# Recurrence feeding a mixture of experts: bonus sums in half as many products, loads cut into pieces and asked for later, and another order of the matmuls in a chunk

## The chip, the cores and the metric

The program runs on 1 core of one Trainium2 chip. The metric is the device time in microseconds (us) of one execution; lower is better.

## What is computed

A linear recurrence over 768 tokens in 4 batches of 8 heads of width 48, and then a mixture of 8 experts with top-1 routing on its output. Cut to what matters:

```
for t in range(S):                                  # attention, per batch and head
    cur = outer(u * k[t], v[t])
    y[t] = r[t] @ (state + cur)                     # (r*u*k) . v is the "bonus"
    state = w[:, None] * state + outer(k[t], v[t])
x = y laid out as 3072 tokens x 384
e = argmax(x @ w_gate); gate = softmax(x @ w_gate)[e]
out[token] = gate * (relu(x @ w1[e]) @ w2[e])       # each expert takes at most 768 tokens
```

## The kernel before

The 3072 tokens are cut into 24 chunks of 128 (`NI`), 6 for each batch, and each chunk into two halves `s` of 64 tokens. Two heads share the 128 partitions (`g`), four such pairs `p` make up the 8 heads. Inside a chunk the recurrence is done with matrix products; one loop, `for i in range(NI)` (L616), works on several chunks at once. It is written out by hand in the order in which every engine takes its instructions. An iteration `i` does, on TensorE:

- `scores(i + 1)` (L396): 16 products of 64 x 64 into the bank `pk`; VectorE then puts them under the diagonal of the tile `s` (`masks`, L405).
- `turn(i - 1)` (L469): three 128 x 128 transposes of the finished chunk `x` (`xpose`, L73) and the three router products of the chunk before that (`gates`, L77), into one bank `xp` of PSUM. ScalarE copies that bank to SBUF (L486).
- `update(i + 1)` (L408): 16 products for the state, into `pu`. VectorE and GpSimd carry the state on (`carry`, L417: L425, L428, L430).
- `advance("t", 1)`: now and then the products of a routing step (`route`, L111: L120, L121, L158).
- `values(i)` (L432): 16 products of the scores with v, into `py`.
- `fill(i, 4)` (L464): four bf16 products of zeros, 128 x 392, into the bank `xp` that `turn(i)` uses in the next iteration. Their results are overwritten.
- `bonus(i + 3)` (L361): for each pair of heads, half and head one product of a 48 x 64 block of `z` = r*k with one column of u; 16 products of one column each, into a corner of the bank `pu`.
- `inter(i)` (L443): 16 products of r with the state, added to `py`. ScalarE copies `py` to the tile `x` (L456), SyncE stores `x` to DRAM two iterations later (`store`, L459).

ScalarE's order in an iteration: copy of the bonus sums (`bon`, L373), eight multiplications that put them on the diagonal of `s` (`diag`, L377), copy of `xp` (L486), a two-column copy `seen` (L446), copy to `x` (L456), and sometimes a cast of expert 0's weights (L219). GpSimd makes `z` (`product`, L355), the state's multiplication (L430) and `kt` (`prep_state`, L389). VectorE makes `kd` and `rt` (L387, L382).

Loads are asked for by SyncE, which takes its transfers strictly in order. `load(i + 5)` (L346) opens the iteration: r and k of a chunk in two transfers to `dm` (4 buffers), k and v in token order in one to `bd` (6 buffers, L353). The transfer to `bd` reuses the buffer that `values(i - 1)` reads. Behind it stand the store of `x` and, in seven of the iterations, a 384 or 512 KB piece of expert 0's weights (`wstream`, L205, L211), and `dm` of the next chunk. In the built program each SyncE transfer also waits for the transfer eight before it.

Before the loop stand constants (`powers`, L526), the loads of five chunks and some runs of filling products (`warm`, L500). After the loop come expert 0's first layer while the last routing steps end, and then the experts one after the other (L265 to L284); nothing of this part changes.

Of the kernel before, what the change touches and what calls it, by code (L numbers as in the profile page):

```python
# [35 lines left out]
def rwkv_moe(nc, tc, dmj, rkv, bdc, wp, wv, uv, wg, w1, w2, out, cap):  # L36
# [3 lines left out]
    with ExitStack() as ctx:  # L40
# [70 lines left out]
        def route(gi, i0, n, l, sm, ps, tp):  # L111
# [74 lines left out]
        with ExitStack() as mc:  # L186
# [18 lines left out]
            def wstream(e, plan):  # L205
                raw = {}

                def fetch(k):
                    r = raw[k] = wrw.tile([128, F if k < 3 else 2 * DM], F32, tag="wr", name=f"wr{k}_{e}")
                    src = w1[e, :, k] if k < 3 else w2[e, :, 2 * k - 6:2 * k - 4].rearrange("p f d -> p (f d)")  # L210
                    nc.sync.dma_start(out=r, in_=src)  # L211
# [117 lines left out]
            wc = wk.tile([PR, NP], F32, name="wc", bufs=1)  # L329
            w128 = wk.tile([PR, NP], F32, name="w128", bufs=1)  # L330
# [8 lines left out]
            pb = pu[:, :, NP * D:NP * D + NP]  # L339
            ftp = pu[0:PR, :, 256:].rearrange("q h (p t) -> q h p t", p=2)  # L340
            xl_ = wk.tile([128, RING, 392], F32, name="xl_", bufs=1)
# [4 lines left out]
            def load(i):  # L346
                b, c = divmod(i, NC)
                t = T[i] = {"dm": dmb[i % 4]}
                q = 64 if i < 4 else D
# [11 lines left out]
            def bonus(i):  # L361
                t = T[i]
                for p in range(NP):
                    for s in range(2):
                        for g in range(2):
                            r, o = slice(64 * g, 64 * g + D), 64 * (g ^ s)
                            nc.tensor.matmul(pb[o:o + 64, s, p:p + 1], lhsT=t["z"][r, p, 64 * s:64 * s + 64],  # L367
                                             rhs=wut[r, 1, p:p + 1], start=True, stop=True)

            def diag(i):  # L370
                t = T[i]
                bon = sm.tile([128, 2, NP], F32, tag="bon", name=f"bon{i}")
                nc.scalar.copy(out=bon, in_=pb)  # L373
                s = t["s"] = wk.tile([128, 2, NP, 64], F32, tag="s", name=f"s{i}", bufs=3)
                for h in range(2):
                    for p in range(NP):
                        nc.scalar.mul(out=s[:, h, p], in_=eye, mul=bon[:, h, p:p + 1])  # L377
# [560 lines left out]
```

## Time and profile before

| | before |
|---|---|
| median of 3 runs | 456.41 us (452.42 to 460.54) |
| the profiled execution | 449.77 us, its span 448.1 us |
| TensorE: matmuls, weight loads | busy 419.6 us (94%), 375.1 us (84%) |
| VectorE, ScalarE, GpSimd | 231.3 us, 191.6 us, 145.8 us |
| data moved | 59.44 MB, mean 133 GB/s |
| mean granted TensorE clock | 0.871 of full speed |

The granted clock has two levels, 1.00 (2.4 GHz) and 0.50 (1.2 GHz). PE is TensorE's matmuls, PEld its weight loads, DVE VectorE, ACT ScalarE, POOL GpSimd, SPq SyncE's queue. A product in f32 is recorded as two matmuls, so the 16 products of a step stand there as x32. In brackets behind a row stands the idle time ahead of it and what ended it; "issue" is time in which the engine waited for nothing that the profile shows.

### The profile page before, as it was taken

How to read it: one execution, taken by the hardware profiler on the slowest of the kernel's cores; microseconds unless marked ns; L12 is line 12 of the kernel's file. 1: busy time of each engine (PE TensorE's matmuls, PEld its weight loads, DVE VectorE, ACT ScalarE, POOL GpSimd, SP SyncE). 2: the span in 40 equal slices, each digit the busy share in tenths (PEclk: the TensorE clock that was granted, in tenths of full speed). 3: DMA queues.
4: the chain of work that ended last, by engine and by line, in shares of the span. 5: the costliest groups of instructions: out<-in, count | busy, mean ns of one | idle time of the engine just before them, and what ended most of it. 6: DMA issues, size and time to landing. Idle time of an engine off the chain costs nothing.

```text
span 448.1 us, 13332 instructions
## 1 busy us (share of the span) xinstructions
PE 419.6 (94%) x5572; PEld 375.1 (84%) x5573; DVE 231.3 (52%) x518; ACT 191.6 (43%) x545; POOL 145.8 (33%) x228
## 2 busy tenths in 40 slices
PE   8779998899987998879999999999999999999994
PEld 4458787778776877778999999999999999999993
DVE  5525534357566696378556445365463553553320
ACT  4425355335353544327337245264263462552402
POOL 4742525362663354026033131330330420200303
PEclk9855569565596599969999999999999999999998
DMA  7966556463464512208545355444553553430101
GB/s 191 239 161 186 163 161 179 136 169 102 140 188 147 146 45 79 68 18 309 159 145 157 102 185 149 143 137 111 158 152 123 147 161 118 123 92 0 53 0 64
DMA packets 22038, 59.44 MB, mean 133 GB/s; under 512 B 3946, under 2 KB 7058, under 8 KB 21968
## 3 DMA queue, kind: packets, MB, share of 16 engines
q1 hardware_dynamic: 18240, 48.85, 39.0%
q0 software_dynamic: 3584, 9.44, 6.1%
q8 instruction: 46, 0.75, 0.8%
q14 instruction: 24, 0.20, 0.1%
q10 hardware_dynamic: 144, 0.20, 0.1%
HBM read 49.38 MB, written 9.78 MB: 132 GB/s over the span
## 4 chain that ended last, share of the span: by engine, by line
PE 64%; issue 21%; DVE 6%; POOL 4%; ACT 3%; POOLq 1%; DVEq 0%
PE b L282 5%; PE xp L467 5%; PE a L266 5%; PE a L265 5%; PE a L267 5%; PE b L283 5%; PE b L284 5%; PE pu L367 4%; PE py L453 4%; PE xp L77 4%; POOL out L291 3%; PE pu L414 3%; PE py L440 3%; PE xp L73 3%; PE pk L402 3%
## 5 line engine op out<-in xcount | busy, mean ns | idle before, releaser
L265 PE MATMUL a<-xh,ws 128*128 128x412 f32 (+1 forms) x216 | 76.1, 352 | 0.1
L220 DVE TENSOR_TENSOR ws<-wr,ws 128x384 fp32r<-128x384 f32 (+1 forms) x112 | 66.5, 612 | 15.0 <-ACT ws L219 14.0
L266 PE MATMUL a<-xl,ws 128*128 128x412 f32 (+1 forms) x216 | 73.4, 340 | 0.5 <-DVE xl L253 0.5
L267 PE MATMUL a<-xh,ws 128*128 128x412 f32 (+1 forms) x216 | 73.1, 338 | 0.0
L282 PE MATMUL b<-hh,ws 128*128 128x412 f32 (+1 forms) x192 | 68.1, 355 | 0.0
L270 ACT ACTIVATE hh<-a 128x412 fp32r<-128x412 f32 (+2 forms) x72 | 34.3, 476 | 77.2 <-PE a L267 77.2
L291 POOL DMA_INDIRECT out<-yo,ids x32 | 31.2, 976 | 109.0 <-ACT yo L290 109.0
L283 PE MATMUL b<-hl,ws 128*128 128x412 f32 (+1 forms) x192 | 65.8, 343 | 0.0
L284 PE MATMUL b<-hh,ws 128*128 128x412 f32 (+1 forms) x192 | 65.7, 342 | 0.0
L271 DVE SCALAR_TENSOR_TENSOR hl<-a,hh 128x412 fp32r<-128x412 f32 (+2 forms) x72 | 38.7, 538 | 46.5 <-ACT hh L270 46.4
L219 ACT CAST ws<-wr 128x384 fp32r<-128x384 f32 (+1 forms) x112 | 59.8, 557 | 0.0
L234 POOL DMA_INDIRECT xg<-x_dr,ids x30 | 30.0, 999 | 87.9 <-PE tp L248 68.2
L285 DVE COPY yt<-b 128x412 f32<-128x412 f32 (+1 forms) x24 | 13.7, 570 | 72.7 <-PE b L284 72.7
L377 ACT ACTIVATE s<-eye,bon 128x64 f32<-128x64 f32 x192 | 48.5, 335 | 0.8
L266 PEld LDWEIGHTS a<-xl,ws 128*128 128x128 f32 x216 | 41.8, 193 | 1.0 <-DVE xl L253 0.9
L265 PEld LDWEIGHTS a<-xh,ws 128*128 128x128 f32 x216 | 41.8, 194 | 0.8 <-ACT xh L252 0.4
L267 PEld LDWEIGHTS a<-xh,ws 128*128 128x128 f32 x216 | 41.6, 193 | 0.1
L456 ACT COPY x<-py 128x384 f32<-128x384 f32 x24 | 11.5, 478 | 64.7 <-PE py L453 55.3
L430 POOL TENSOR_TENSOR st<-q,w 112x192 f32<-112x192 f32 x20 | 11.9, 597 | 83.2 <-DVE q L428 46.1
L359 POOL TENSOR_TENSOR z<-dm 112x256 f32<-112x256 f32 x48 | 35.2, 755 | 6.8 <-DMA dm<-dmj 5.2
L282 PEld LDWEIGHTS b<-hh,ws 128*128 128x128 f32 x192 | 36.1, 188 | 0.9
L406 DVE COPY_PREDICATED s<-msk,pk 128x512 f32<-128x512 int32 x24 | 17.7, 736 | 36.6 <-PE pk L402 31.7
(145 smaller groups left out, 691.5 us busy)
## 6 DMA issues: line engine op xcount, KB each, us to landing
wr<-w SPq DMA_DIRECT2D x24, 512.0 KB, 3.6
wr<-w SPq DMA_DIRECT2D x32, 384.0 KB, 3.4
bd<-bdc SPq DMA_DIRECT2D x24, 384.0 KB, 3.6
dm<-dmj SPq DMA_DIRECT2D x44, 192.0 KB, 5.6
x_dr<-x SPq DMA_DIRECT2D x23, 192.0 KB, 3.6
dm<-dmj SPq DMA_DIRECT2D x4, 256.0 KB, 8.2
out<-yo,ids POOLq DMA_INDIRECT x32, 2.8
xg<-x_dr,ids POOLq DMA_INDIRECT x30, 3.3
```

The costliest lines, as they stand in the source:

```text
L219: nc.scalar.copy(out=hi, in_=r)
L220: nc.vector.tensor_tensor(out=lo, in0=r, in1=hi.bitcast(F32), op=ALU.subtract)
L265: nc.tensor.matmul(o, lhsT=wh, rhs=xh[:, d, a:z], start=d == 0, stop=False)
L266: nc.tensor.matmul(o, lhsT=wh, rhs=xl[:, d, a:z], start=False, stop=False)
L267: nc.tensor.matmul(o, lhsT=wl, rhs=xh[:, d, a:z], start=False, stop=d == 2)
L271: nc.vector.scalar_tensor_tensor(out=hl[:, f, b:z], in0=o[:, b - a:], scalar=0.0, in1=hh[:, f, b:z].bitcast(F32), op0=ALU.max, op1=ALU.sub ...
L282: nc.tensor.matmul(o, lhsT=wh, rhs=hh[:, f, :n], start=f == 0, stop=False)
L283: nc.tensor.matmul(o, lhsT=wh, rhs=hl[:, f, :n], start=False, stop=False)
L284: nc.tensor.matmul(o, lhsT=wl, rhs=hh[:, f, :n], start=False, stop=f == 7)
L291: r = nc.gpsimd.indirect_dma_start(out=out[:, :], out_offset=bass.IndirectOffsetOnAxis(ap=ids[:q, at:at + 1], axis=0), in_=yo, in_offset=N ...
L359: nc.gpsimd.tensor_tensor(out=z[:, p:p + 2], in0=t["dm"][:, 0, p:p + 2], in1=t["dm"][:, 1, p:p + 2], op=ALU.mult)
L377: nc.scalar.mul(out=s[:, h, p], in_=eye, mul=bon[:, h, p:p + 1])
```

## The change

The bonus sums are made by 8 products in place of 16: all 112 partitions of `z` (both heads) times two columns (`uz`, u of one head in each, zeros elsewhere). For that the layout of r and k on the host swaps the halves of the second head, and the tiles that depend on it (`ft`, `kb`, `s`) are indexed to fit. The sums go to eight columns of the bank `xp` next to the transposes, and the one copy of that bank (400 columns in place of 392) takes them along; the copy `bon` falls away, except for the first four chunks, which have a bank and a copy of their own. `turn` no longer follows `fill` by an iteration: three filling products of 400 columns, the transposes and the router products now come in a row, behind `update`. The copy of the bank follows `bonus` (`keep_turn`). Loads come in six transfers for each chunk (four of 96 KB to `dm`, two of 192 KB to `bk` and `bv`), each where the buffer that it fills has been read, up to seven chunks ahead; expert 0's weights come in halves of 64 partitions, at most two in an iteration. `x` is stored one iteration after it is made. A routing step of the first groups waits one iteration more before its products (`yield "v"`). The setup makes the powers of w in a tile of their own (some small VectorE instructions more).

```
+            if i0 + n < SNAP:
+                yield "v"
...
+                        later.extend([(r[64 * h:64 * h + 64], src[64 * h:64 * h + 64]) for h in range(2)])
...
-                nc.sync.dma_start(out=t["dm"][0:q], in_=dmj[b, c, 0:q])
-                nc.sync.dma_start(out=t["dm"][64:PR], in_=dmj[b, c, D:])
-                bd = t["bd"] = ld.tile([128, 2, 8, D], F32, tag="bd", name=f"bd{i}", bufs=6)
-                nc.sync.dma_start(out=bd, in_=bdc[b, c])
...
+                if j < 2:
+                    q = 64 if i < 4 else D
+                    nc.sync.dma_start(out=t["dm"][0:q, j], in_=dmj[b, c, j, 0:q])
+                    nc.sync.dma_start(out=t["dm"][64:PR, j], in_=dmj[b, c, j, D:])
+                else:
+                    k, bufs = (("bk", 4), ("bv", 6))[j - 2]
+                    n = t[k] = ld.tile([128, 8, D], F32, tag=k, name=f"{k}{i}", bufs=bufs)
+                    nc.sync.dma_start(out=n, in_=bdc[b, c, j - 2])
...
-            def bonus(i):
...
+            def bonus(i, o):
+                z = T[i]["z"]
                 for p in range(NP):
-                    for s in range(2):
-                        for g in range(2):
-                            r, o = slice(64 * g, 64 * g + D), 64 * (g ^ s)
-                            nc.tensor.matmul(pb[o:o + 64, s, p:p + 1], lhsT=t["z"][r, p, 64 * s:64 * s + 64],
-                                             rhs=wut[r, 1, p:p + 1], start=True, stop=True)
+                    for h in range(2):
+                        q = slice(64 * h, 64 * h + 64)
+                        nc.tensor.matmul(o[q, 2 * p:2 * p + 2], lhsT=z[:, p, q], rhs=uz[:, p], start=True, stop=True)
+
+            def bonus_alone(i):
+                m = ps1.tile([128, 8], F32, tag="xp", name=f"pb{i}")
+                bonus(i, m)
+                b = T[i]["bon"] = sm.tile([128, 8], F32, tag="bon", name=f"bon{i}", bufs=4)
+                nc.scalar.copy(out=b, in_=m)
...
-                bon = sm.tile([128, 2, NP], F32, tag="bon", name=f"bon{i}")
-                nc.scalar.copy(out=bon, in_=pb)
...
-                m = turns[i] = ps1.tile([128, 392], F32, tag="xp", name=f"xp{i}")
+            def turn(i, n):
+                m = T.setdefault(i, {})["m"] = ps1.tile([128, 400], F32, tag="xp", name=f"xp{i}")
...
-                    nc.tensor.matmul(m, lhsT=wz[:, 0:128], rhs=wz[:, 0:392], start=True, stop=True)
...
+                hi = 8
+                if i < NI:
+                    hi = 392
+                if i + 4 < NI:
+                    hi = 400
+                    T[i + 4]["bon"] = xl_[:, k, 384:392]
...
             for i in range(NI):
-                each(load, i + 5)
-                if i >= 2:
-                    store(i - 2, nc.sync)
+                if i >= 1:
+                    store(i - 1, nc.sync)
+                part()
                 each(product, i + 3)
                 each(diag, i + 2)
                 each(scores, i + 1)
+                each(update, i + 1)
                 if i >= 1:
-                    turn(i - 1)
-                each(update, i + 1)
+                    turn(i - 1, 3)
                 each(masks, i + 1)
                 each(prep_k, i + 3)
+                each(load, i + 7, 1)
                 each(carry, i + 1)
                 each(prep_r, i + 3)
+                each(prep_state, i + 3)
+                each(load, i + 7, 2)
+                each(load, i + 7, 0)
+                part()
                 advance("t", 1)
                 values(i)
-                fill(i, 4)
-                each(bonus, i + 3)
+                each(load, i + 6, 3)
+                if i >= 1:
+                    if i + 3 < NI:
+                        bonus(i + 3, T[i - 1]["m"][:, 392:])
+                else:
+                    bonus_alone(3)
+                seen(i)
+                if i >= 1:
+                    keep_turn(i - 1)
                 inter(i)
-                each(prep_state, i + 3)
                 advance("v")
                 if i >= 1:
                     next(more, None)
...
                 next(ws)
```

TensorE in one iteration of the loop before (the products of chunks 11 and 12; `xp_2044` is the bank that the next iteration's transposes go to):

```order
L77 MATMUL xp_1904<-wgs,xl__139 128x8 x3
L414 MATMUL pu<-bd_1412,kt_1805 48x48 x16
L440 MATMUL py<-bd_1278,s_1699 64x48 x16
L467 LDWEIGHTS wz
L467 MATMUL xp_2044<-wz 128x392
...
L367 MATMUL pu<-wut,z_1966 64x1 x16
L453 MATMUL py<-st_12_1881,rt_118 64x48 x8
L402 MATMUL pk<-rt_120,kd_124 64x64 x16
L73 MATMUL xp_2044<-idn,x_2075 128x128 x3
L77 MATMUL xp_2044<-wgs,xl__139 128x8 x3
```

and TensorE in one iteration of the changed kernel:

```order
L414 MATMUL pk<-rt_121,kd_122 64x64 x16
L425 MATMUL pu<-bv_1591,kt_1969 48x48 x16
L478 LDWEIGHTS wz
L478 MATMUL xp_2200<-wz 128x400
...
L73 MATMUL xp_2200<-idn,x_2135 128x128 x3
L77 MATMUL xp_2200<-wgs,xl__142 128x8 x3
...
L451 MATMUL py<-bv_1468,s_1907 64x48 x16
L376 MATMUL xp_2200<-uz,z_2156 64x2 x8
L466 MATMUL py<-st_14_1966,rt_120 64x48 x2
```

The update (L414, now L425) stands behind the scores, the filling products between it and the transposes, and the bonus (L367, now L376) right behind the values.

ScalarE in one iteration before:

```order
L446 COPY seen_1925<-py 128x2
L456 COPY x_1943<-py 128x2x4x48
L373 COPY bon_1969<-pu 128x8
L377 ACTIVATE s_1971<-eye,bon_1969 128x64 x8
L486 COPY xl__139<-xp_1904 128x392
```

and of the changed kernel:

```order
L455 COPY seen_2002<-py 128x2
L501 COPY xl__142<-xp_1948 128x400
L469 COPY x_2013<-py 128x2x4x48
L389 ACTIVATE s_2020<-eye,xl__142 128x64 x8
```

The copy of the bank `xp` (L486, now L501) has moved from behind the eight multiplications to ahead of the copy to `x`.

SyncE in one iteration before:

```order
L353 DMA bd_2229<-bdc 128x768
L460 DMA x_dr<-x_2075 128x384
L211 DMA wr_0_2364<-w 128x768
L350 DMA dm_114<-dmj 48x1024
```

and of the changed kernel:

```order
L473 DMA x_dr<-x_1012 128x384
L647 DMA wr_0_1015<-w 64x1024
L358 DMA dm_114<-dmj 48x512
L359 DMA dm_114<-dmj 48x512
L363 DMA bk_1086<-bdc 128x384
...
L363 DMA bv_1107<-bdc 128x384
```

Transfers are half as large and twice as many; the one into `bv` stands alone behind the values.

## Rows read from the trace of the kernel before

**Rows 1.** The page's head: the profiled execution's span.

```profile
span 448.1 us, 13332 instructions
```

**Rows 2.** Busy time of each engine in stretches of the span, cut where the granted clock changes: us, busy us (and instructions) of PE, PEld, DVE, ACT, POOL, then the clock, the mean busy share of the DMA engines and GB/s.

```profile
30.70:63.20 32.50, 32.50 (x686) 26.65 (x684) 14.82 (x27) 13.01 (x49) 12.40 (x27) 0.50 0.56 158
63.20:76.90 13.70, 11.91 (x435) 10.34 (x434) 5.54 (x11) 7.28 (x28) 8.81 (x16) 1.00 0.72 210
76.90:90.60 13.70, 11.81 (x252) 9.34 (x252) 6.91 (x14) 5.92 (x23) 4.61 (x9) 0.50 0.46 123
90.60:94.00 3.40, 2.58 (x104) 2.32 (x104) 2.12 (x7) 1.34 (x6) 1.92 (x10) 1.00 0.86 264
94.00:121.30 27.30, 27.30 (x565) 22.37 (x567) 16.60 (x35) 12.01 (x47) 13.23 (x21) 0.50 0.43 114
121.30:138.40 17.10, 14.09 (x477) 11.90 (x477) 12.42 (x29) 10.29 (x38) 12.44 (x23) 1.00 0.66 197
138.40:158.80 20.40, 19.44 (x392) 15.71 (x392) 12.43 (x28) 7.11 (x27) 5.32 (x12) 0.50 0.46 128
158.80:184.60 25.80, 22.98 (x746) 18.99 (x745) 17.01 (x54) 11.77 (x43) 9.23 (x17) 1.00 0.23 73
```

**Rows 3.** The chain of work that ended last, 46 to 54 us, in order of time: start us, us, what.

```profile
46.28 1.42 PE xp L467 x4
47.70 0.96 PE pu L367 x32
48.66 0.93 PE py L453 x32
49.59 0.88 PE pk L402 x32
50.47 0.83 PE xp L73 x3
51.30 1.08 PE xp L77 x6
...
54.05 0.44 PE xp L467
```

**Rows 4.** TensorE's timeline, 61 to 74 us: start us, us, instruction, idle time before.

```profile
61.76 1.49 PE L467 MATMUL xp<-wz 128*128 128x392 bf16 x4
63.18 0.66 PE L367 MATMUL pu<-wut,z 48*64 48x1 f32 x32
63.69 0.65 PE L453 MATMUL py<-st,rt 48*64 48x48 f32 x32
...
66.39 0.65 PE L440 MATMUL py<-bd,s 64*64 64x48 f32 x32
67.44 0.82 PE L467 MATMUL xp<-wz 128*128 128x392 bf16 x4 [0.40 <-ACT seen L446]
...
72.96 0.82 PE L467 MATMUL xp<-wz 128*128 128x392 bf16 x4 [0.40 <-ACT seen L446]
```

**Rows 5.** ScalarE's timeline in the same chunk.

```profile
69.94 0.48 ACT L456 COPY x<-py 128x384 f32<-128x384 f32 x1 [2.50 <-PE py L453]
70.31 0.17 ACT L373 COPY bon<-pu 128x8 f32<-128x8 f32 x1
70.52 2.02 ACT L377 ACTIVATE s<-eye,bon 128x64 f32<-128x64 f32 x8
72.44 0.46 ACT L486 COPY xl__139<-xp 128x392 f32<-128x392 f32 x1
72.81 0.15 ACT L446 COPY seen<-py 128x2 f32<-128x2 f32 x1
```

**Rows 6.** What TensorE waited for in the loop, 30.7 to 184.6 us: us in total, times, longest.

```profile
PE t L158 <- DVE at L152: 2.3, 1, 2.3
PE pu L414 <- issue: 1.9, 1, 1.9
PE py L453 <- issue: 1.3, 3, 0.7
PE pk L402 <- issue: 1.3, 2, 0.9
PE xp L467 <- ACT seen L446: 0.8, 2, 0.4
...
PE pu L367 <- issue: 0.3, 1, 0.3
```

**Rows 7.** TensorE's instructions by line and shape: the bonus (records, busy us, mean ns of one, idle before and what ended it).

```profile
L367 PE MATMUL pu<-wut,z 48*64 48x1 f32 x768 | 20.4, 218 | 5.6 <-issue 4.2 <-DVE rt L382 0.7 <-POOL st L430 0.5
```

**Rows 8.** What SyncE's queue waited for from 14 to 185 us, longest first: us in total, times, longest.

```profile
SPq L353 <- PE py L440: 87.8, 17, 7.2
```

**Rows 9.** The page's DMA queues, the one that brings instructions: packets, MB, the time that their packets took as a share of 16 engines' span.

```profile
q8 instruction: 46, 0.75, 0.8%
```

**Rows 10.** Two short stretches of the span, with the columns of Rows 2.

```profile
76.00:78.00 2.00, 1.89 (x35) 1.87 (x35) 1.40 (x3) 1.97 (x9) 0.49 (x1) 0.73 0.71 188
78.00:80.00 2.00, 0.20 (x6) 0.04 (x1) 0.50 (x1) 1.05 (x4) 0.00 (x0) 0.50 0.00 0
```

**Rows 11.** SyncE's timeline behind one iteration's end: the transfers that it asks for in a row.

```profile
81.40 0.35 SPq L353 DMA_DIRECT2D bd<-bdc  x1
...
83.97 0.44 SPq L351 DMA_DIRECT2D dm<-dmj  x1
```

More of the change, by code (lines that the diff above doesn't have):

```diff
@@ L203, in wset, with wstream @@
                 return wtiles[e]
-            def wstream(e, plan):
+            def wstream(e, plan, later=None):
                 raw = {}
@@ L210, in fetch @@
                     src = w1[e, :, k] if k < 3 else w2[e, :, 2 * k - 6:2 * k - 4].rearrange("p f d -> p (f d)")
-                    nc.sync.dma_start(out=r, in_=src)
+                    if later is None:
+                        nc.sync.dma_start(out=r, in_=src)
+                    else:
+                        later.extend([(r[64 * h:64 * h + 64], src[64 * h:64 * h + 64]) for h in range(2)])
                 def split(n):
@@ L393, in prep_state @@
                 for q in range(0, 8, 4):
[L394 removed]
+                    (eng or nc.gpsimd).tensor_tensor(out=kt[:, q:q + 4], in0=t["bk"][:, q:q + 4], in1=kf[:, q:q + 4], op=ALU.mult)
             def scores(i):
@@ L439, in values, with seen @@
                             a = 64 * (g ^ s)
-                            nc.tensor.matmul(y[64 * s:64 * s + 64, g, cs], lhsT=t["s"][a:a + 64, s, p], rhs=t["bd"][a:a + 64, 1, 2 * p + s],
+                            nc.tensor.matmul(y[64 * s:64 * s + 64, g, cs], lhsT=t["s"][a:a + 64, g, p], rhs=t["bv"][a:a + 64, 2 * p + s],
                                              start=p == 0, stop=p == NP - 1 and t[f"s{s}"] is None)
+            def seen(i):
+                nc.scalar.copy(out=sm.tile([128, 2], F32, tag="seen", name=f"seen{i}"), in_=py[:, :, 200])
             def inter(i):
@@ L445, in inter @@
                 y = t["y"]
-                nc.scalar.copy(out=sm.tile([128, 2], F32, tag="seen", name=f"seen{i}"), in_=y[:, :, 200])
                 for p in range(NP):
@@ L509, in rwkv_moe @@
             for i in range(3):
-                load(i)
+                for j in range(4):
+                    load(i, j)
+            nc.vector.memset(pw[:, :, 0:1], 1.0)
+            nc.vector.memset(sc, 1.0)
+            nc.vector.memset(uz, 0.0)
             nc.vector.memset(pu[:, :, 0:256], 0.0)
@@ L536, in powers @@
                     sq = t
-                nc.scalar.copy(out=kb[:, :, 0:64], in_=ft[:, :, 127:63:-1])
-                rc = sup.tile([PR, NP], F32, name="rc")
-                nc.vector.reciprocal(out=rc, in_=sq)
-                nc.vector.tensor_tensor(out=ft[:, :, 0:64], in0=ft[:, :, 64:], in1=rc.unsqueeze(2).broadcast_to([PR, NP, 64]), op=ALU.mult)
-                nc.scalar.copy(out=kb[:, :, 64:], in_=ft[:, :, 63::-1])
+                for g in range(2):
+                    r = slice(64 * g, 64 * g + (64, D)[g])
+                    nc.vector.reciprocal(out=sc[r, g], in_=sq[r])
+                for h in range(2):
+                    nc.vector.tensor_tensor(out=ft[:, :, 64 * h:64 * h + 64], in0=pw,
+                                            in1=sc[:, h].unsqueeze(2).broadcast_to([PR, NP, 64]), op=ALU.mult)
+                for h in range(2):
+                    nc.scalar.copy(out=kb[:, :, 64 * h:64 * h + 64], in_=ft[:, :, 127 - 64 * h:(63 - 64 * h if h == 0 else None):-1])
                 nc.vector.tensor_tensor(out=w128, in0=sq, in1=sq, op=ALU.mult)
@@ L586, in rwkv_moe @@
             prep_k(0, kb)
+            for g in range(2):
+                r = slice(64 * g, 64 * g + D)
+                nc.vector.tensor_copy(out=uz[r, :, g], in_=wut[r, 1])
             warm(6)
@@ L589, in rwkv_moe @@
             keys()
-            bonus(0)
+            bonus_alone(0)
             warm(3)
@@ L600, in rwkv_moe @@
             warm(9)
-            bonus(1)
+            bonus_alone(1)
             masks(0)
@@ L605, in rwkv_moe @@
             prep_state(1)
-            load(3)
+            for j in range(4):
+                load(3, j)
             prep_k(2)
@@ L609, in rwkv_moe, with part @@
             warm(8)
-            bonus(2)
+            bonus_alone(2)
             prep_state(2)
-            load(4)
+            for i in range(4, 7):
+                for j in range(4):
+                    if i + j < 9:
+                        load(i, j)
             nc.sync.dma_start(out=wgs, in_=wg)
-            ws = wstream(0, PLAN0)
+            parts = []
+            def part():
+                if parts:
+                    r, src = parts.pop(0)
+                    nc.sync.dma_start(out=r, in_=src)
+            ws = wstream(0, PLAN0, parts)
             more = setup3()
             for i in range(NI):
-                each(load, i + 5)
-                if i >= 2:
-                    store(i - 2, nc.sync)
+                if i >= 1:
+                    store(i - 1, nc.sync)
+                part()
                 each(product, i + 3)
@@ L641, in rwkv_moe @@
                 next(ws)
-            store(NI - 2, nc.sync)
+            while parts:
+                part()
             store(NI - 1, nc.scalar)
```

73 lines of the change are left out of this document (36 added, 37 removed).

## The prediction

> **What bounds the kernel now.** The profiled execution took 449.8 us with a span of 448.1 us [rows 1]. I cut the span where TensorE's granted clock changes [rows 2]. From 184.6 us on stand the experts, and nothing there is touched. What can move is the chunk loop, 30.7 to 184.6 us: 153.9 us for 22 of the 24 chunks (the first two run beside the setup and its loads).
>
> The reader should see two regimes in it. At a clock of 0.50 stand 32.5 + 13.7 + 27.3 + 20.4 = 93.9 us, and TensorE is busy for all of them but 2.9: there TensorE itself is the bound. The chain of waits shows one such chunk [rows 3]: from one group of filling products to the next 54.05 - 46.28 = 7.77 us, of which fill 1.42, bonus 0.96, inter 0.93, scores 0.88, transposes 0.83, gates 1.08, and update and values the remaining 1.67. (93.9 - 2.9) / 7.77 makes 11.7 chunks at half clock. The other 10.3 chunks share the 60.0 us at full clock, 5.8 us each, and there TensorE is not full: 51.6 us busy.
>
> What it waits for at full clock is a loop through ScalarE. From fill to fill 72.96 - 67.44 = 5.52 us [rows 4], and the fill waits each time 0.40 us, put down to `seen`. ScalarE's rows say why [rows 5]: the copy to `x` starts at 69.94, then come `bon`, eight multiplications of 2.02 us, the copy of the bank `xp`, and `seen`, which ends at 72.96, when the fill starts. The fill needs that bank; bonus and inter stand behind the fill, and the next `x` behind inter. The last view, TensorE's waits in the loop [rows 6], has two more things: 4.8 us of "issue" (1.9 + 1.3 + 1.3 + 0.3), and 2.3 us in which the routing products stand waiting for `at`, and everything behind them too.
>
> **The change part by part.** Fill. Three products of 400 columns for four of 392: 1.42 x 1200 / 1568 = 1.09 us at half clock, so -0.33; at full clock 0.82 becomes 0.63, -0.19.
>
> Bonus. Half as many products suggest half of 0.96 us. I don't count that. The bonus streams one column and takes 0.96 us for 32 records, the scores stream 64 and take 0.88 for 32 [rows 3]: the price is that of a product, not of its columns. And products overlap: a record lasts 218 ns in the mean [rows 7], and 32 of them are done in 0.66 us [rows 4], since four neighbours lie in the four quarters of the array. So 32 records are 8 rounds of four. The new products fill all rows and half of the columns: 16 records, two side by side, again 8 rounds. I take 0.96 as before, difference 0. Bounds: by the record, 16 x 0.03 = 0.48 us; and if no two overlap, 16 records at the price of a record of the gates (1.08 / 6 = 0.18 us, with twice the columns of weights) 2.88 us. Half of that, 1.44, is the likelier form of the bad case.
>
> The Trainium skill, on the page "TensorE: Matmul & The Clock Gate", section on packing small matmuls, says that a weight load runs beside a matmul in flight only where their row groups differ. The new products all use the same rows, so by that rule the two halves would wait for each other, at the 1.44 us of the bad case. The rows on the quarters neither prove nor exclude it, as two of four neighbours there do have different rows.
>
> The order. Scores, update, fill, transposes, gates, values, bonus, inter. The bank `xp` is now free when the copy behind the last bonus has ended, so the fill no longer closes the loop through ScalarE. The transposes need `x`; ahead of them stand scores, update and fill, at half clock 0.88 + some 0.8 + 1.09 us, at full clock some 1.5, while the copy takes 0.48 [rows 5]. So it is covered; without the cover it would cost its 0.5 to 0.9 us a chunk. ScalarE's own sum, 0.48 + 2.02 + 0.46 + 0.15 = 3.1 us a chunk (the copy `bon`, 0.17, gone), and VectorE and GpSimd, with 5.5 and 8.8 us in a stretch of 13.7 with two and a half chunks [rows 2], stay below TensorE. So a chunk at full clock costs TensorE's work: 63.18 to 67.04 (67.44 less the wait of 0.40) is all but the fill, 3.86 us [rows 4]; with a fill of 0.63 and less small gaps 4.4 us. At half clock 7.77 - 0.33 = 7.44 us.
>
> Loads. The same bytes. SyncE now stands 87.8 us at the transfer to `bd`, which waits for values [rows 8]; then that, the store, weights and `dm` go out within 3 us [rows 11]. In the loop no product waits long for these data, so an earlier request gains nothing by itself. What the bursts may cost is code: 46 transfers of instructions, 0.75 MB [rows 9], share the DMA engines with them. TensorE's longest "issue" in the loop falls into 78 to 80 us, right behind a stretch of busy DMA (0.71), with nothing else late [rows 10]. Smaller pieces, and 17 of some 173 records fewer in a chunk, speak for shorter waits; a shorter chunk brings them closer together. Now they are 4.8 / 10.3 = 0.47 us for a full-clock chunk; I count 0.6 with all small gaps. Bounds: 0 and 1.0. SyncE has some 8 transfers a chunk at 0.35 to 0.44 us [rows 11], 3.3 us, which fits. Each waits for the eighth before it, which halves what is in flight; four chunks of lead hide that.
>
> The page "Runtime: NRT & Kernel Launch" of the Trainium skill, section "Instruction fetch mechanics", calls the price of crossing a block of instructions mostly hidden. Here it isn't, if the waits are what I take them for; if the page holds for this loop, they have another cause and stay, and the sum is some 2 us worse.
>
> Routing. The extra step before the products of the first groups takes the 2.3 us away [rows 6]; the step itself costs nothing, since the table is needed chunks later. Setup. Some VectorE instructions and twice the transfers to issue ahead of the first scores: +1 us (0 to 2).
>
> The clock. It decides more than all of this: a chunk is 2.4 us shorter at full clock. It rose at 63.2 us right behind values and fill [rows 2, 4]; it fell at 138.4, in the wait for `at`, and at 76.9, just ahead of the longest "issue" [rows 2, 10]. The new order puts inter, scores, update and fill in one run and takes waits away, but has a quarter less fill. I take 13 of the 22 chunks at full clock, for 10.3 now.
>
> **Sum.** 9 x 7.44 + 13 x (4.4 + 0.6) + 1.5 us of waits left at half clock = 133.5 us for 153.9: -20.4, with the setup -19.4, so 430.4 in place of 449.8. That execution lies 6.6 us under the median of the runs shown (456.4); carried over, 437.0.
>
> **Rivals**, in terms of the median. Full clock nearly throughout once it has risen, since chunks have no gaps left: 4 x 7.44 + 18 x 5.0 = 119.8, so -33: 423; with 4.6 for a chunk 416. For it: falls came beside waits, and one of these goes. Against: the waits for code don't vanish.
>
> The clock never rises in the loop with a fill a quarter smaller: 22 x 7.44 = 163.7, with the setup +10.8: 467. That is the one on the other side. It decides from 4.4 full-clock chunks down (163.7 - 2.44 n = 152.9). For it: with all four products the clock stayed low for 32.5 us of busy TensorE [rows 2]. Against: the run of products ahead of the fill gets longer.
>
> No gain to speak of: 11.7 chunks at half clock as now, and at full clock the waits for code fill what ScalarE's loop leaves, 5.4 us a chunk: 145.5 with all 2.9 us of waits, so -7.4: 449. For it: a denser TensorE asks for code and data faster, and the DMA share at full clock is 0.66 to 0.86 already, but for the last stretch [rows 2].
>
> The two halves of the bonus wait for each other: 9 x 7.92 + 13 x 5.4 + 1.5 = 143, so -10: 446; at the gates' price 470.
>
> **Numbers.** Forecast 0.47 (own range 428 to 446), full clock throughout 0.14, never 0.15, no gain 0.16, bonus 0.08. A difference of 2%, 9 us, is about what a measurement of this kernel can tell. Under 447: nearly all of the first two and a third of the last, 0.62. Over 465: most of "never" and the top of the bonus, 0.15. Between: 0.23. Below 412 the cases leave 0.03, above 462 some 0.14: that is the range.
>
> **What would show it.** Right: at half clock 7.4 us from fill to fill; the 16 records of the bonus in 0.9 to 1.0 us; at full clock a chunk of 5 us without waits for `seen`; the wait for `at` gone; "issue" in the loop not above 8 us. Wrong: a bonus of 1.4 us or more; a loop at 0.50 with no rise; or "issue" growing as fast as the chunk shrinks.

## The result, and the profile after

The changed kernel takes 425.56 us in the median of four runs (420.60 to 430.67) beside 458.48 us for the kernel before (452.42 to 460.59): ratio 0.933, 95% interval 0.915 to 0.951. It is faster, inside the predicted range, and 11.4 us under the forecast 437.0. The profiled execution took 424.96 us. Ratios and comparisons here leave disturbed runs out (over 1.5% above the fastest of their kernel), so 0.933 is not the quotient of the two medians, and where too few runs remain for an interval the text gives the plain median of the undisturbed ones and their number. From the profiles of two experiments (loads alone, bonus alone) only the start is drawn on for causes.

The page of the changed kernel, its head and the queue that brings instructions (packets, MB, share), beside [rows 1, 9]:

```profile
span 423.3 us, 12656 instructions
...
q8 instruction: 42, 0.69, 0.7%
```

The span is 24.8 us shorter. One instruction cuts it into three parts in either kernel: ScalarE's copy to `x`, once a chunk. Kernel before, the instructions of that line (durations min/median/max, first and last start), and the second of them from ScalarE's timeline:

```profile
L456 ACT COPY x<-py x24: 478/478/479, 25.7 to 184.9; 128x384 f32<-128x384 f32 x24
```

```profile
34.13 0.48 ACT L456 COPY x<-py 128x384 f32<-128x384 f32 x1 [3.20 <-PE py L453]
```

The same two views of the changed kernel:

```profile
L469 ACT COPY x<-py x24: 479/479/481, 20.4 to 158.0; 128x384 f32<-128x384 f32 x24
```

```profile
27.93 0.48 ACT L469 COPY x<-py 128x384 f32<-128x384 f32 x1 [0.60 <-PE py L466]
```

So the start (to the second copy) went from 34.1 to 27.9 us, -6.2; the 22 chunks from there to the last copy from 150.8 to 130.1, -20.7; the rest from 448.1 - 184.9 = 263.2 to 423.3 - 158.0 = 265.3, +2.1. Sum -24.8. The prediction had +1, -20.4 and 0. Its loop began at 30.7 us, so its 133.5 for 153.9 us and the 130.1 for 150.8 here are stretches cut differently: only the differences compare.

The loop, cut where the granted clock changes, with the columns of [rows 2]:

```profile
27.93:31.55 3.62, 3.62 (x74) 3.06 (x66) 2.65 (x7) 2.39 (x9) 0.71 (x3) 0.50 0.80 239
31.55:38.38 6.83, 6.42 (x248) 5.93 (x251) 5.71 (x9) 3.69 (x13) 4.31 (x8) 1.00 0.73 219
38.38:41.79 3.41, 3.41 (x64) 2.85 (x55) 3.34 (x8) 2.40 (x10) 3.41 (x7) 0.50 0.77 202
41.79:48.62 6.83, 5.75 (x205) 5.27 (x205) 2.65 (x6) 3.20 (x12) 2.21 (x5) 1.00 0.94 236
48.62:69.10 20.48, 20.48 (x415) 18.37 (x411) 7.73 (x16) 9.49 (x33) 8.27 (x16) 0.50 0.84 208
69.10:79.34 10.24, 8.64 (x300) 7.92 (x300) 7.25 (x17) 6.76 (x24) 6.19 (x16) 1.00 0.59 152
79.34:86.16 6.82, 6.51 (x151) 5.55 (x151) 4.18 (x10) 3.57 (x12) 5.04 (x10) 0.50 0.66 193
86.16:99.82 13.66, 12.22 (x444) 11.12 (x446) 12.00 (x27) 7.33 (x27) 9.60 (x14) 1.00 0.67 179
99.82:127.12 27.30, 27.30 (x496) 24.54 (x486) 17.93 (x39) 12.70 (x45) 11.45 (x20) 0.50 0.59 171
127.12:144.19 17.07, 15.42 (x514) 13.86 (x518) 14.87 (x43) 9.42 (x35) 10.59 (x22) 1.00 0.31 96
144.19:147.60 3.41, 3.41 (x100) 2.85 (x101) 1.57 (x5) 2.84 (x11) 1.20 (x3) 0.50 0.17 59
147.60:158.00 10.40, 9.32 (x278) 8.11 (x277) 4.04 (x20) 2.79 (x11) 2.75 (x3) 1.00 0.40 109
```

Half clock holds 65.0 us of it, TensorE idle for 0.3; full clock another 65.0 us, TensorE busy for 57.8. What a chunk costs at either, in TensorE's timeline (beside [rows 3, 4]):

```profile
59.31 1.18 PE L478 MATMUL xp<-wz 128*128 128x400 bf16 x3
...
62.15 1.11 PE L451 MATMUL py<-bv,s 64*64 64x48 f32 x32
63.19 1.02 PE L376 MATMUL xp<-uz,z 112*64 112x2 f32 x16
64.13 1.11 PE L466 MATMUL py<-st,rt 48*64 48x48 f32 x32
...
66.69 1.18 PE L478 MATMUL xp<-wz 128*128 128x400 bf16 x3
...
71.98 0.68 PE L478 MATMUL xp<-wz 128*128 128x400 bf16 x3
...
73.49 0.68 PE L451 MATMUL py<-bv,s 64*64 64x48 f32 x32
74.10 0.63 PE L376 MATMUL xp<-uz,z 112*64 112x2 f32 x16
74.67 0.68 PE L466 MATMUL py<-st,rt 48*64 48x48 f32 x32
...
76.12 0.68 PE L478 MATMUL xp<-wz 128*128 128x400 bf16 x3
```

At half clock a chunk takes 66.69 - 59.31 = 7.38 us, and its bonus 64.13 - 63.19 = 0.94 us with 16 records, for 0.96 with 32 [rows 3]. Those two stand in different orders and views; the like comparison is "all but the bonus" below. At full clock this chunk takes 76.12 - 71.98 = 4.14 us, and no fill waits for `seen`. (65.0 - 0.3) / 7.38 = 8.8 chunks at half clock leave 13.2 for the 65.0 us at full clock: 4.93 each, of which TensorE works 57.8 / 13.2 = 4.38.

TensorE's waits in the loop of the changed kernel, 28 to 158 us (us in total, times, longest), beside [rows 6]:

```profile
PE rk L121 <- POOL lane L117: 1.7, 1, 1.7
PE xp L376 <- POOL z L369: 1.6, 3, 1.1
PE xp L77 <- issue: 1.1, 1, 1.1
PE py L466 <- ACT seen L455: 1.0, 3, 0.4
...
PE xp L376 <- issue: 0.4, 1, 0.4
```

The wait of 2.3 us for `at` is gone, "issue" fell from 4.8 to 1.5 us, and a wait for GpSimd's `lane` (running sums of the routing) has taken first place. With the two rows left out (0.8 us for `rt`, 0.5 for `kd`) the waits come to 7.1 us. So of TensorE's 65.0 - 57.8 = 7.2 idle us at full clock only 1.5 are issue.

### The profile page after: what moved, and what is told of

Same layout as the page of the kernel before. It is cut to its first block, busy times and chain, and to the rows that moved or that the text cites. A ratio compares the mean times of both kernels' runs of the same rounds, so it can differ in the third digit from the quotient of the medians.

```text
span 423.3 us, 12656 instructions
## 1 busy us (share of the span) xinstructions
PE 402.0 (95%) x5161; PEld 370.7 (88%) x5162; DVE 229.8 (54%) x524; ACT 189.7 (45%) x525; POOL 146.3 (35%) x228
## 4 chain that ended last, share of the span: by engine, by line
PE 60%; issue 21%; POOL 6%; DVE 6%; SPq 3%; ACT 1%; DMA 1%; POOLq 1%; ACTq 0%; DVEq 0%
PE b L287 6%; PE a L271 5%; PE a L270 5%; PE a L272 5%; PE b L288 5%; PE b L289 5%; PE xp L478 4%; PE py L466 4%; PE xp L77 3%; POOL out L296 3%; PE py L451 3%; PE pk L414 3%; PE xp L376 3%; PE pu L425 2%; PE xp L73 2%
## 5 line engine op out<-in xcount | busy, mean ns | idle before, releaser
L270 PE MATMUL a<-xh,ws 128*128 128x412 f32 (+1 forms) x216 | 77.1, 357 | 0.1
L225 DVE TENSOR_TENSOR ws<-wr,ws 128x384 fp32r<-128x384 f32 (+1 forms) x112 | 68.5, 630 | 15.1 <-ACT ws L224 14.3
L271 PE MATMUL a<-xl,ws 128*128 128x412 f32 (+1 forms) x216 | 74.3, 344 | 0.5 <-DVE xl L258 0.5
L272 PE MATMUL a<-xh,ws 128*128 128x412 f32 (+1 forms) x216 | 74.1, 343 | 0.0
L271 PEld LDWEIGHTS a<-xl,ws 128*128 128x128 f32 x216 | 42.8, 198 | 1.0 <-DVE xl L258 0.8
L270 PEld LDWEIGHTS a<-xh,ws 128*128 128x128 f32 x216 | 42.7, 198 | 0.6 <-ACT xh L257 0.4
L272 PEld LDWEIGHTS a<-xh,ws 128*128 128x128 f32 x216 | 42.6, 197 | 0.1
L389 ACT ACTIVATE s<-eye,xl__142 128x64 f32<-128x64 f32 x160 | 40.4, 337 | 0.0
L287 PEld LDWEIGHTS b<-hh,ws 128*128 128x128 f32 x192 | 36.1, 188 | 0.9
L289 PEld LDWEIGHTS b<-hh,ws 128*128 128x128 f32 x192 | 36.2, 188 | 0.2
L288 PEld LDWEIGHTS b<-hl,ws 128*128 128x128 f32 x192 | 36.1, 188 | 0.1
L257 ACT CAST xh<-tp 128x412 fp32r<-128x412 f32 (+2 forms) x27 | 12.4, 469 | 52.4 <-PE tp L253 52.2
```

The costliest lines, as they stand in the source:

```text
L225: nc.vector.tensor_tensor(out=lo, in0=r, in1=hi.bitcast(F32), op=ALU.subtract)
L270: nc.tensor.matmul(o, lhsT=wh, rhs=xh[:, d, a:z], start=d == 0, stop=False)
L271: nc.tensor.matmul(o, lhsT=wh, rhs=xl[:, d, a:z], start=False, stop=False)
L272: nc.tensor.matmul(o, lhsT=wl, rhs=xh[:, d, a:z], start=False, stop=d == 2)
L287: nc.tensor.matmul(o, lhsT=wh, rhs=hh[:, f, :n], start=f == 0, stop=False)
L288: nc.tensor.matmul(o, lhsT=wh, rhs=hl[:, f, :n], start=False, stop=False)
```

## The experiments

Three things are bundled: loads, order and bonus; the setup's new tables and the earlier store of `x` have no run of their own. First each alone or left out, then the clock and the code. "Loop" is from the first copy to `x` to the last, 159.2 us before and 137.6 now.

**Loads alone**, on the kernel before. Because `bk` is asked for where it comes free, `prep_state` moves ahead too.

```diff
-                each(load, i + 5)
-                if i >= 2:
-                    store(i - 2, nc.sync)
+                if i >= 1:
+                    store(i - 1, nc.sync)
+                part()
...
+                each(load, i + 7, 1)
...
+                each(prep_state, i + 3)
+                each(load, i + 7, 2)
+                each(load, i + 7, 0)
+                part()
```

> The kernel before with the new loads alone (pieces of 192 KB and less, asked for where each buffer comes free; the weights in halves); bonus, fill and order as before. Theory 1 (the bursts of large loads delay instruction code, so the loads explain the earlier start and the fewer issue waits): the first copy to x starts near 20.5 us for 25.7, TensorE's issue waits up to the experts fall from 10 us to under 5, and the time is 7 to 12 us shorter, ratio 0.973 to 0.985. Rival (the order, not the loads, took them away; the loads are hidden anyway): first copy to x at 25 to 26, ratio 0.995 to 1.005.

Measured: 446.2 us (1 run) beside 458.2 (3 runs), ratio 0.974 without an interval: with one run the size stays open. The first copy to `x` starts at 21.7 us, the second at 29.3 (34.1 before). TensorE's waits from 14 to 30 us, with the kernel before (14 to 34 us) for comparison:

```profile
PE pu L373 <- DVE rt L388: 1.7, 2, 1.1
PE py L446 <- issue: 0.6, 1, 0.6
PE pu L373 <- issue: 0.5, 1, 0.5
```

```profile
PE pu L367 <- issue: 3.8, 2, 2.4
PE py L440 <- issue: 1.3, 1, 1.3
```

The loads end most of the issue waits of the start, 5.1 us for 1.1. That the issue waits up to the experts fall under 5 us, as theory 1 also had it, isn't borne out: 5.0 + 2.0 + 0.7 = 7.7 us stand from 30 to 188 us of this one profile. DMA there, in the stretch 15 to 25 us of before and of this kernel (columns of [rows 2]):

```profile
15.00:25.00 10.00, 5.67 (x178) 3.97 (x176) 2.53 (x5) 3.14 (x14) 6.87 (x12) 0.69 1.05 244
```

```profile
15.00:25.00 10.00, 7.63 (x276) 6.25 (x275) 5.27 (x12) 5.73 (x24) 7.52 (x14) 0.83 0.77 223
```

**Order alone**, on the kernel before.

```diff
-                    turn(i - 1)
-                each(update, i + 1)
+                each(update, i + 1)
+                if i >= 1:
+                    turn(i - 1, 4)
...
-                fill(i, 4)
                 each(bonus, i + 3)
+                seen(i)
+                if i >= 1:
+                    keep_turn(i - 1)
                 inter(i)
```

> The kernel before with the new order of TensorE alone (update ahead of the transposes, fill and transposes in one turn, the copy of the bank behind values and bonus); four fill products, 32 bonus products and loads as before. Theory 1 (the order takes away the loop through ScalarE at full clock and nothing at the start): first copy to x still at 25.7, no waits of the fill for seen, a chunk at full clock 5.0 to 5.3 us for 5.8, loop 8 to 14 us shorter, ratio 0.968 to 0.983. Rival (the order also takes the issue waits away and explains nearly all): ratio under 0.95. Second rival (the order moves nothing, since the waits for code fill what the loop left): 0.99 to 1.0.

Measured: 446.8 us (2 runs) beside 458.2 (3 runs), 0.975; first copy to `x` at 27.4 us, loop 151.0. As the first theory had it, no fill waits for `seen`, and the first copy to `x` comes no earlier. But the chunk at full clock did not fall to 5.0 to 5.3 us. From the second copy to the last (33.1 to 178.4 us) half clock holds 78.5 us, TensorE idle for 2.3; at 7.44 to 7.50 us from fill to fill that is 10.2 chunks, and the other 11.8 share 66.8 us, 5.7 each (an estimate from these rows). A new wait took the old one's place, the update for ScalarE's copy `bon` (3.2 us, seven times), and issue grew to 8.6 us (28 to 179 us).

**Bonus alone**, on the kernel before: halves, in the transposes' bank, with the table layouts they need and with the setup's new way to make these tables.

```diff
-                            nc.tensor.matmul(pb[o:o + 64, s, p:p + 1], lhsT=t["z"][r, p, 64 * s:64 * s + 64],
-                                             rhs=wut[r, 1, p:p + 1], start=True, stop=True)
+                        nc.tensor.matmul(o[q, 2 * p:2 * p + 2], lhsT=z[:, p, q], rhs=uz[:, p], start=True, stop=True)
...
+                    nc.scalar.copy(out=t["bon"], in_=T[i - 3]["m"][:, 392:])
```

> The kernel before with the new bonus alone (8 products of half an array into the transposes' bank, its sums copied by ScalarE at the head of the next chunk; the table layouts that go with it; four fill products of 400 columns); order and loads as before. Theory A (the form is worth nothing, and the place pays only with the new order, since in the old order no product waits at the bank of the update): ratio 0.985 to 1.005. Theory B (the new bonus helps by itself, through fewer instructions to fetch): first copy to x at 21 to 22 us for 25.7, ratio 0.965 to 0.98.

Measured: 447.3 us (1 run) beside 451.3 (1 run), 0.991 without an interval: it can't be told from no change. The first copy to `x` starts at 22.5 us, 3.2 earlier and just outside theory B's 21 to 22; the whole stays with A. Whether the earlier start is due to fewer instructions, as theory B says, or to the setup's changes isn't shown, as this kernel has both.

**All but the loads.**

> The changed kernel with the loads of before (one transfer for both halves of dm, one of 384 KB for k and v, the weights whole, all asked for at the head of a chunk). Theory 1 (loads and order each give their part): first copy to x back at 25 to 26 us, issue waits back to 8 us or more, ratio to before 0.955 to 0.968, against 0.933 for the changed kernel. Rival (order alone): 0.93 to 0.94 and issue waits near 3 us.

```diff
+                nc.sync.dma_start(out=t["dm"][0:q], in_=dmj[b, c, 0:q])
+                nc.sync.dma_start(out=t["dm"][64:PR], in_=dmj[b, c, D:])
...
+                nc.sync.dma_start(out=bd, in_=bdc[b, c])
...
-            ws = wstream(0, PLAN0, parts)
+            ws = wstream(0, PLAN0)
...
+                each(load, i + 5)
+                if i >= 2:
+                    store(i - 2, nc.sync)
```

Measured: ratio 0.953 (0.947 to 0.960), just outside theory 1's range; this interval and that of the changed kernel (0.915 to 0.951) overlap, so the loads' share of some 2% is not clear of noise. The first copy to `x` stands at 21.3 us, not at 25: either the new loads or the new bonus with its setup is enough for it, and their gains don't add up. The second copy comes at 30.2 us, 2.3 later than in the changed kernel. The loop takes 144.7 us, with 4.5 + 1.8 + 1.4 + 0.4 + 0.3 = 8.4 us of issue from 28 to 166 us.

**All but the bonus**: quarters, in the update's banks.

```diff
-                        nc.tensor.matmul(o[q, 2 * p:2 * p + 2], lhsT=z[:, p, q], rhs=uz[:, p], start=True, stop=True)
+                            nc.tensor.matmul(pb[q, g, p:p + 1], lhsT=z[r, p, q], rhs=wut[r, 1, p:p + 1], start=True, stop=True)
...
+                nc.scalar.copy(out=bon, in_=pb)
```

> The changed kernel with the bonus of before: 16 products of a quarter array each, in the banks of the state update, with a copy of their sums on ScalarE; all else changed. Theory 1 (eight rounds either way): 32 records in 0.95 us at half clock and 0.55 to 0.66 at full clock, ratio to before 0.925 to 0.945, the same as the changed kernel. Rival (half the products is half the price, the halves cost what a product costs): bonus 0.5 us dearer in each chunk, some 11 us, ratio 0.95 to 0.96.

Measured: 0.985 (0.972 to 0.997), loop 155.9 us. Both theories fail. The quarters are not dearer but cheaper, as TensorE's timeline shows, first at half and then at full clock:

```profile
66.88 1.11 PE L449 MATMUL py<-bv,s 64*64 64x48 f32 x32
67.77 0.99 PE L378 MATMUL pu<-wut,z 48*64 48x1 f32 x32
68.61 1.08 PE L464 MATMUL py<-st,rt 48*64 48x48 f32 x32
...
70.91 0.89 PE L423 MATMUL pu<-bv,kt 64*48 64x48 f32 x32 [0.33 <-ACT bon L383]
...
81.65 0.68 PE L449 MATMUL py<-bv,s 64*64 64x48 f32 x32
...
82.61 0.68 PE L464 MATMUL py<-st,rt 48*64 48x48 f32 x32
```

The bonus takes 68.61 - 67.77 = 0.84 us, where the halves take 0.94. From the start of the values to the start of inter it is 68.61 - 66.88 = 1.73 us with quarters and 64.13 - 62.15 = 1.98 with halves at half clock, 0.96 and 1.18 at full clock. So in this order the new form costs TensorE 0.22 to 0.25 us a chunk, some 5 us in 22 chunks (an estimate). But the update behind the quarters waits for `bon` (4.1 us, 13 times). So the time is lost elsewhere: either the form counts in a way that I hadn't seen, or the place does.

**The changed kernel again**, as a mark in the same job.

> The changed kernel once more, as the mark for the other three on this chip: ratio to before 0.92 to 0.95, first copy to x near 20.4 us, the last near 158, bonus 0.94 to 0.96 us at half clock.

423.7 us (2 runs) beside 454.5 (2 runs), 0.932; loop 20.2 to 154.5 us, 134.3. Between two executions of one kernel the loop differs by 3 us, with the clock's pattern: from the second copy to the last, full clock holds 65.0 of 130.1 us in the first and some 80 of 127.0 us in this one (its mean clock there is 0.82).

**The new form in the old place**: 8 products of half an array into the update's bank, copied by ScalarE at the head of the next chunk.

```diff
+            pb = pu[:, 0, NP * D:NP * D + 8]
...
-                        bonus(i + 3, T[i - 1]["m"][:, 392:])
+                each(bonus, i + 3)
```

> The changed kernel with the bonus in its new form (8 products of half an array), but in the bank of the state update, copied by ScalarE at the head of the next chunk, as before; order, loads and fill as changed. Theory A (the place counts: in the new order the bonus waits for VectorE's reads of the update, and the update for ScalarE's copy of the bonus): waits of the bonus and the update at this bank of 8 us or more, ratio 0.97 to 0.99, as for the quarter products there (0.985). Theory B (the form counts, fewer records): ratio 0.93 to 0.945, as for the changed kernel, and no such waits.

Measured: 0.972 (0.952 to 0.993), loop 147.6 us. TensorE's waits from 21 to 169 us:

```profile
PE pu L422 <- ACT bon L382: 4.6, 14, 0.7
PE pu L377 <- POOL st L438: 3.4, 2, 3.2
...
PE pu L377 <- DVE ps L125: 0.5, 1, 0.5
```

Theory A: the place, though the interval's lower end, 0.952, lies near theory B's 0.945. 4.6 + 3.4 + 0.5 = 8.5 us of the 10.0 to 13.3 by which the loop is longer than in the two executions of the changed kernel. With the update right behind the scores, the copy `bon` at the head of the chunk is no longer done when the update wants the bank; and the bonus wants it while VectorE, busy with routing, hasn't yet read that bank in `carry` and for `rt` (the profile puts this down to GpSimd's `st`, which ends at about the same time). In the old order the transposes and the gates stood between scores and update, and no wait of the loop is for `bon` [rows 6]. The quarters lose another 8 us of loop in one execution, although their products are cheaper; they have 7.3 us of issue for 1.8 here. The two intervals overlap, and no run has the quarters in the new bank, so what the form is worth as a whole stays open.

**The fill**: none, and six products.

```diff
-                    turn(i - 1, 3)
+                    turn(i - 1, 0)
```

and in the other kernel `turn(i - 1, 6)`.

> The changed kernel without any fill product in the loop (the products compute nothing that is used). Theory A (the fill is what brings the clock up): half clock through the whole loop, 23 chunks of 6.4 us = 147 us from the first copy to x to the last, for 138 now, ratio near 0.955. Theory B (the other products hold the clock as well): as much full clock as now, 0.98 us saved in some 10 chunks and 0.5 us in some 13, 16 us, ratio near 0.90.

> The changed kernel with six fill products in place of three. Theory A (more fill keeps the clock up): full clock for most of the loop, chunks of 5.5 us, 23 x 5.5 = 127 us, 11 us less than now, ratio near 0.91. Theory B (the clock does not follow the fill): 0.98 us more in some 10 chunks and 0.5 us in some 13, 16 us more, ratio near 0.97.

Without fill: 0.954 (0.938 to 0.971), copies to `x` from 21.0 to 169.4 us, 148.4 for an expected 147. Three stretches of that loop:

```profile
21.00:70.00 49.00, 48.18 (x1134) 46.00 (x1126) 25.37 (x49) 24.23 (x87) 26.01 (x51) 0.52 0.81 212
70.00:120.00 50.00, 48.87 (x1161) 46.86 (x1158) 35.93 (x78) 26.79 (x95) 29.19 (x55) 0.57 0.56 161
120.00:169.00 49.00, 46.16 (x1018) 44.06 (x1021) 25.01 (x76) 18.58 (x66) 17.12 (x31) 0.50 0.34 100
```

The clock is 0.50 to 0.57: theory A. The filling products, which compute nothing, are what brings full clock in this loop. With six: 421.8 us (2 runs) beside 454.5 (2 runs), 0.928, loop 134.0 us at a clock of 1.00, 0.72 and 0.98 in its thirds, and neither theory: the clock comes as A says, and the time doesn't. Most of what it gives the fill itself takes: three more products at the 0.52 us that three take at full clock (71.98 to 72.50 us in the changed kernel) are some 11 us in 22 chunks, an estimate. Another part goes into issue, 4.3 + 1.1 + 0.9 + 0.9 + 0.5 + 0.2 = 7.9 us from 28 to 155 us; without fill there is none from 27 to 169 us.

**No loads from chunk 8 on.**

```diff
-                if j < 2:
+                if i >= 8:
+                    if j >= 2:
+                        k = ("bk", "bv")[j - 2]
+                        t[k] = old[k, i % (4, 6)[j - 2]]
+                elif j < 2:
```

> The changed kernel without the loads of chunks 8 to 23, which compute with the data of earlier chunks in the same buffers (so the outputs are not the reference's), and with the flags of the slow path set to zero; weights, stores and instructions as they are. Theory A (issue waits are code that the loads' transfers delay): TensorE's issue waits from 40 us to the end of the loop are under 1 us, for 1.5 to 5 us in the two runs of the changed kernel, although the clock is full as often. Theory B (code comes late by itself when TensorE runs at full clock): issue waits of 2 us or more stay.

Loop 20.8 to 157.9 us, 137.1, as with all loads. The stretch of it without loads, and what TensorE waited for as "issue" there, from the timeline:

```profile
40.00:158.00 118.00, 110.46 (x3003) 99.55 (x3003) 76.01 (x185) 61.25 (x218) 62.34 (x112) 0.76 0.22 67
```

```profile
145.27 0.67 PE L483 MATMUL xp<-wz 128*128 128x400 bf16 x3 [1.28 <-issue]
```

Between the theories: 1.3 us, with a DMA share of 0.22, where the changed kernel had 1.1 us at 0.74 and 0.45 (40 to 100, and 100 to 158 us), and 3.5 us from 40 us on in its second execution. In this one execution, then, the loads cost the loop nothing that can be seen.

**Without the extra routing step.**

```diff
-            if i0 + n < SNAP:
-                yield "v"
```

> The changed kernel without the extra routing step ahead of the products of the first groups. Theory A (the step takes the wait away): TensorE waits 1 to 2.5 us for at in the loop, as before (2.3 us), and one look cannot tell it in the time, 422 to 432 us. Theory B (the new order alone hides it): no such wait in the loop.

One execution, 429.0 us. TensorE's waits, 28 to 160 us, first row:

```profile
PE t L158 <- DVE at L152: 2.2, 2, 1.9
```

As theory A had it, in one execution; the changed kernel has no such row in its loop, nor has the second execution. But the order alone, which lacks the step too, has no wait for `at` in its loop either. So the step is not shown to be what takes the wait away: it may come and go with the timing.

**More fill, most of it early.**

```diff
-                    turn(i - 1, 3)
+                    turn(i - 1, 6 if i < 12 else 4)
```

> The changed kernel with six fill products in the chunks up to the twelfth and four in the rest. Theory A (the clock that six products held from the start, at three of them lost after 33 us, is worth more than their columns): the clock stays full to 60 us or beyond, 3 to 6 us less than the changed kernel, ratio to before 0.905 to 0.92. Theory B (what the clock gives, the fill takes): ratio 0.92 to 0.935.

424.4 us (5 runs) beside 451.3 (1 run), ratio 0.940 without an interval and in neither theory's range; beside the 425.0 (3 runs) of the changed kernel there is no gain that can be told. The clock comes as theory A says (0.93 in the mean from 21 to 70 us, for 0.65), and the loop does gain, 21.1 to 149.5 us, 128.4 for 137.6, 9.2 less. The stretch behind it, 271.0 us for 265.3, takes 5.7 of that back; first this kernel, then the changed one:

```profile
149.50:180.00 30.50, 24.96 (x133) 23.06 (x134) 17.09 (x65) 10.21 (x30) 11.10 (x14) 0.67 0.34 113
180.00:420.50 240.50, 233.70 (x1334) 225.32 (x1332) 112.18 (x215) 100.19 (x214) 51.30 (x52) 0.99 0.39 117
```

```profile
158.00:188.00 30.00, 27.35 (x174) 25.85 (x174) 21.48 (x76) 13.91 (x40) 11.09 (x14) 0.77 0.41 133
188.00:423.30 235.30, 228.56 (x1293) 220.21 (x1291) 107.49 (x205) 96.25 (x203) 51.32 (x52) 0.99 0.40 118
```

In its first 30 us after the loop TensorE finishes 133 instructions for 174, at a clock of 0.67 for 0.77 and with 5.5 us without work for 2.7. Beside the second execution of the changed kernel (loop 134.3 us, 265.9 behind it) 5.1 of 5.9 us are given back. The transition to the experts is the next place to work on.

## Why the prediction was right, and where it was not

**Half-clock chunk**: 7.44 predicted, 7.38 measured. **Full-clock chunk**: 5.0 predicted as 4.4 of work and 0.6 of waits; 4.93 measured, as 4.38 and 0.55. The size of the waits is luck: 0.6 was meant as issue and small gaps, and most of the 0.55 are waits for other engines. The 0.47 behind it was also misread: 1.9 of the 4.8 us of issue, at 78 to 80 us, stand at half clock [rows 10]. **The clock**: 13 of 22 chunks predicted, 13.2 measured. That is luck too, as no sum gave the 13: in the second execution it is nearly 16 by the same working, and the loop is 3.3 us shorter. So the loop's -20.4 met -20.7 with the regimes right and some of the sizes by chance. The rival that the clock never rises was a real one: without fill it is what happens. That three products are enough, the prediction could not know.

**The bonus, difference 0**: the 0.9 to 1.0 us came, as 0.94. The rival that its halves wait for each other, at 1.44 us, fell; by the rule of the Trainium skill (page "TensorE: Matmul & The Clock Gate", section on packing small matmuls) they would have, and the trace disagrees. Yet the step was incomplete, twice. In one and the same order the halves cost 0.22 to 0.25 us a chunk more than quarters, which the comparison with the old order hid. And I priced the products and not their bank. The new order needs the bonus to leave the update's bank: with loads and order but the old place, 0.972 (halves) or 0.985 (quarters), with the new place 0.933. So the new products win nothing by themselves, and their place carries over half of the gain by these figures, whose intervals nearly meet. The prediction's sum came out since it took the order's gain with the new bank and didn't ask what the order is worth without it.

**The order**: right where the bank is free. No fill waits for `seen`, and no transposes wait for `x` in the loop of the first execution (2.1 us, once, in the second); what replaced them is 1.0 us of inter for `seen`. Alone it left the full-clock chunk at 5.7 us, which the prediction didn't ask about. **The wait for `at`**: gone, and back at 2.2 us without the step; but the order alone, which has no such step, shows no such wait either.

**The setup, +1 us (0 to 2)**: this term failed. It measured -6.2. I counted the instructions that the change adds ahead of the first scores, and took the waits that stood there for given: 5.1 us of issue up to 34 us. The loads alone bring the first copy to `x` from 25.7 to 21.7 us, the bonus with its setup alone to 22.5, both with the order to 20.4. At the second copy, where the -6.2 is measured, it is 34.1 before, 29.3 with the loads alone, 32.0 with the bonus alone, 30.2 with all but the loads and 27.9 with all: there the loads count most.

**The experts, unchanged**: +2.1 us. In the 30 us behind the last copy to `x` TensorE does 174 instructions at a clock of 0.77; in the kernel before it does 188 at 0.89 (184.9 to 214.9 us). The sum took the clock's gain in the loop and no change of it behind.

**The median**: I carried 6.6 us from the profiled execution to the median, since before's lies that far below it. After's lies 0.6 below its own. These 6.0 us, and the 5.4 us of the three parts of the span (-7.2 at the start, -0.3 in the loop, +2.1 behind it), are the 11.4 us by which 437.0 was too high.

**Issue as code delayed by bursts**: not above 8 us, as predicted (1.5 here; 1.8 + 1.1 + 0.6 + 0.6 = 4.1 in the second execution). That the loads' bursts cause it is not shown. For it: with the large loads, 8.4 us in the same order. Against: with no loads 1.3 us stay, and with the new loads and quarters there are 7.3, so loads are not all of it. What the rows do show is that most of it begins at full clock: none in the loop without fill, 7.9 us with six products. The Trainium skill's "mostly hidden" (page "Runtime: NRT & Kernel Launch", section "Instruction fetch mechanics") agrees with the loop at half clock and, if these waits are code, not with that at full clock. That they are code at all stays an inference.

## What to carry to other kernels

When work moves on an in-order engine, list who else uses the banks it passes: the same products cost 4% more in one bank than in another (0.972 and 0.932, in one job), and an order can show its worth only once the bank is free. Compare the price of a new form with the old one in the same order, not across orders. Look at the waits that already stand where a change adds instructions, not only at what it adds. And time that is won in a stretch with a changing clock has to be followed to the end of the span: here 5.7 of 9.2 us of loop were given back behind it.

## What the runs showed that I had not expected

- Products in all rows and half of the columns each run in little more time than twice as many quarters: 16 records of 112 x 64 in 0.94 us, 32 of 48 x 64 in 0.84 us, at half clock and behind the same values. The values ahead of them reach the next group later too (63.19 - 62.15 = 1.04 us for 0.89), so half the products were a small loss.
- Products that compute nothing made the kernel faster: three of them a chunk shorten the loop from 148.4 to 137.6 us, although they take 0.98 us of TensorE at half clock (59.31 to 60.29 us). Six of them raise the clock further and shorten nothing more (134.0 us, beside 134.3 for three in the same job); six in half of the chunks and four in the rest give 128.4 us, but most of that gain is lost again behind the loop.
- Issue waits of TensorE mostly begin at full clock: 0 and 7.9 us in two kernels whose loops differ only in filling products. There are exceptions, such as the longest one of the kernel before [rows 10].
